# Moving the first dense half's weight conversion from the attention loop to expert slots 1 to 6

## The chip, the cores and the metric

One core of one Trainium2 chip runs the whole program. The metric is the device time in microseconds (us) of one execution; lower is better. Engines are named as the profile names them: PE is TensorE (matmul), PEld its weight load, DVE is VectorE, ACT is ScalarE, POOL is GpSimd, and SP is SyncE, which issues DMAs here. One core shares its DMA engines among all its queues.

## The reference

Three layers follow each other. The inputs of the first two are fp32; the two weight arrays of the last, `w_in` and `w_out`, are fp64.

```python
# attention: 4 batches x 12 heads, 448 tokens, head size 64, causal
scores = mask(scale * (q @ k.T)); attn = softmax(scores); x = attn @ v      # x: [1792, 768]
# mixture of experts: 8 experts, 768 -> 1024 -> 768, one expert for each token
e = argmax(x @ w_gate); gate = softmax(x @ w_gate)[e]
x[t] = gate[t] * (relu(x[t] @ w1[e[t]]) @ w2[e[t]])
# dense layer, 768 -> 2048 -> 768
h = x @ w_in; out = (h - tanh(h)) @ w_out
```

## The kernel before, in words

Every matmul that matters runs on pairs of fp32 tiles: `split` (L152 on ACT for the high part, L154 on DVE for the low part) makes `hi` and `lo`, and three products are summed.

**Attention** goes over 24 pairs of heads. One pass of `for p in range(1, NPAIR + 1)` works on several pairs at once: scores of pair `p` (`attend`), row maxima of pair `p+2` (`rowmax`, a DVE reduction at L489 for each block), turned q and k of pair `p+3` (`turn`, `turn_lo`), and the output of pair `p-1` (`divisor`, `values`, `output`). `divisor` makes `rs`, one over the row sums, on DVE (L568, L570). `output` multiplies the values into PSUM (`po`, L588), evicts them with eight ACT instructions of 112x64 that scale by `rs` (`x_sb`, L595), and evicts the gate logits with two DVE instructions of 112x32 (`tl`, L597). Its PSUM tiles are those that `weigh` and `total` of the next pass need.

**The conversion.** The dense layer's fp64 weights are turned into fp32 by whole-number arithmetic on 32-bit words. The class `Convert` does this in jobs; each has a load (`cv_raw`, SP queue, L96), a `work` step (one ACT square at L108, one POOL compare at L109, three DVE shifts and masks at L110, L112, L114), a `finish` step (one POOL multiply, L126) and a store (SP queue, L135). The first dense half (1024 of the 2048 hidden columns, arrays `win_dr` and `wout_dr[0]` in DRAM) is converted in attention: 42 jobs (18 of 344 or 336 columns, 24 of 256), one in `convert(2p)` and one in `convert(2p+1)` of each pass until they are done. The second half is converted in the dense stage, which the change leaves as it is but for how tiles are got.

**Expert slots.** Tokens are sorted by expert into slots of 128 rows; 18 slots have work here. A slot gathers its rows (POOL, L222), multiplies by `w1` in two halves (`ph0`, `ph1`, L854), applies `relu` (ACT, L859), turns the result (`hturn`, PE L865, then a split), multiplies by `w2` (L874), turns the rows of the next slot (`xturn`), and evicts `ysb` with the gate (ACT, L919), which the next slot stores (POOL, L841). Weights come through four ring buffers `raw0` to `raw3`. `fetch1` loads the next expert's `w1` on the SP queue (L143) where the next change of expert brings one, and then issues, on POOL's queue, four loads of `win_dr` under the condition that the last expert has been reached. `fetch2` does the same for `w2` (L147), with a conditional POOL load of `wout_dr[0]` for the first group. A load whose condition is false moves no bytes, but its engine still waits until the ring buffer is free and the earlier load has landed. `resplit` splits newly loaded weights under a condition read from registers. Expert 0 covers slots 0 to 4; the expert changes at slots 5 and 7 in the stretch that the change touches. After slot 2, `order1` computes tables for the dense layer, most of it on POOL (L998, L1000).

**What sets the order.** The program order of this code is the order on each engine: every engine runs its own list in order, an instruction that waits holds all behind it, and that holds for the queues of SP and POOL too.

**The dense layer** reads the expert output by token, turns it into two tiles `yt` (pool `ytp`, two buffers), and runs both halves. The two `yt` tiles are first written in slot 12.

Of the kernel before, what the change touches and what calls it, by code (L numbers as in the profile page):

```python
# [8 lines left out]
F32 = mybir.dt.float32  # L9
# [18 lines left out]
def fused_kernel(ctx, tc, q, k, v, wg, w1, w2, win, wout, out):  # L28
# [56 lines left out]
    class Convert:  # L85
        def __init__(self, pool, width, same):
            self.pool, self.width, self.same, self.jobs = pool, width, same, []
            self.loaded, self.worked, self.finished, self.stored = 0, 0, 0, 0
            self.raw, self.half, self.res = {}, {}, {}

        def load(self, eng):
            if self.loaded < len(self.jobs):
                src = self.jobs[self.loaded][0]
                raw = self.pool.tile([128, self.width, 2], I32, tag="cv_raw", name="cv_raw")
                raw = raw[:, 0:src.shape[1], :]
                eng.dma_start(out=raw, in_=src)  # L96
                self.raw[self.loaded] = raw
                self.loaded += 1

        def work(self):  # L100
            if self.worked < self.loaded:
# [3 lines left out]
                hi, lo = raw[:, :, 1], raw[:, :, 0]  # L105
                a = self.pool.tile([128, self.width], I32, tag="cv_a", name="cv_a")[:, 0:n]
                m = self.pool.tile([128, self.width], F32, tag="cv_m" if self.same else "cv_h", name="cv_m")[:, 0:n]
                nc.scalar.activation(out=m, in_=hi.bitcast(F32), func=AF.Square)  # L108
# [10 lines left out]
        def finish(self):  # L119
            if self.finished < self.worked:  # L120
                m, a = self.half.pop(self.finished)
                src, dst, on_chip = self.jobs[self.finished]
                h = m
                if not self.same:
                    m = self.pool.tile([128, self.width], F32, tag="cv_m", name="cv_m")[:, 0:src.shape[1]]
                nc.gpsimd.tensor_tensor(out=dst if on_chip else m, in0=h, in1=a.bitcast(F32), op=ALU.mult)  # L126
                self.res[self.finished] = m
                self.finished += 1
# [240 lines left out]
    with ExitStack() as actx:  # L369
        ap1 = actx.enter_context(tc.tile_pool(name="ap1", bufs=1))  # L370
        ap2 = actx.enter_context(tc.tile_pool(name="ap2", bufs=2))
        cvp = actx.enter_context(tc.tile_pool(name="cvp", bufs=2))
        xsp = actx.enter_context(tc.tile_pool(name="xsp", bufs=2))
# [199 lines left out]
        def output(i):  # L573
# [40 lines left out]

        CW = 344
        cv = Convert(cvp, CW, False)
        for kk in range(KD):
            for c0 in range(0, F, CW):
                c1 = min(c0 + CW, F)
                cv.jobs.append((win[kk * 128:(kk + 1) * 128, c0:c1, :],  # L620
                                win_dr[kk * 128:(kk + 1) * 128, c0:c1], False))
        for kk in range(KF):
            for c0 in range(0, DM, 256):
                cv.jobs.append((wout[kk * 128:(kk + 1) * 128, c0:c0 + 256, :],
                                wout_dr[0, kk * 128:(kk + 1) * 128, c0:c0 + 256], False))
        N0 = (B - 1) * H
        cv_by = [max(0, min(len(cv.jobs), n + 3)) for n in range(-4, NHEAD + 2)]

        def convert(n):
            while cv.finished < cv.worked:  # L630
                cv.finish()
            while cv.stored < cv.finished:
                cv.store(nc.sync)
            while cv.worked < cv_by[n]:
                cv.work()
            while cv.loaded < cv_by[n + 2]:
                cv.load(nc.sync)

        e0_t = {}
# [76 lines left out]
        for p in range(1, NPAIR + 1):  # L716
# [7 lines left out]
            maxrow(p + 1)  # L724
            convert(2 * p)
            turn(p + 3, 1)
# [8 lines left out]
            turn_lo(p + 3, 0)  # L735
            convert(2 * p + 1)
            if p + 5 < NPAIR:
# [4 lines left out]
        for n in range(NHEAD - 3, NHEAD):  # L742
            store(n)
        assert cv.stored == len(cv.jobs)

# [40 lines left out]
    with ExitStack() as mctx:  # L786
# [24 lines left out]

# [25 lines left out]
        def slot(s):  # L837
# [86 lines left out]
        def tables():  # L924
# [43 lines left out]
            nc.vector.tensor_copy(rg["more"], hn)  # L968
            nc.vector.tensor_tensor(out=rg["fin"], in0=chg, in1=hn, op=ALU.subtract)

# [71 lines left out]
    with ExitStack() as dctx:  # L1042
        dp = dctx.enter_context(tc.tile_pool(name="dp", bufs=2))
        dio = dctx.enter_context(tc.tile_pool(name="dio", bufs=2))
        pbs = [dio.tile([128, DM], F32, name=f"pb{i}", bufs=1) for i in range(NTT)]
        cv = Convert(dctx.enter_context(tc.tile_pool(name="cvd", bufs=2)), HALF, True)
        assert NHALF == 2
# [205 lines left out]
```

## Time and profile before

| what | us |
|---|---|
| runs before (3), median | 1143.76 (1140.94 to 1148.23) |
| the profiled execution | 1142.36 |
| its span | 1140.9 |
| PE busy in the span | 1069.3 (94%) |
| DVE busy | 776.0 (68%) |
| ACT busy | 590.7 (52%) |
| POOL busy | 481.3 (42%) |
| mean granted clock of the core | 0.982 |

The profiled execution lasts 1.46 us longer than its span; the span runs from the first to the last recorded instruction. Attention's passes fill the stretch from 36 to 301 us of the span, slot 0 the stretch from 301 to 324, slots 1 to 17 follow with some 18.4 us each up to 646, and the dense layer takes the rest. A matmul's record lasts until its modelled end, so a busy PE is not PE at its peak. The granted clock is a share of full speed: 1.00 is 2.4 GHz, and a row between 0.5 and 1.00 mixes both levels.

### The profile page before, as it was taken

What the parts mean: (1) busy time and instruction counts of PE and PEld (TensorE: products, weight loads), DVE (VectorE), ACT (ScalarE), POOL (GpSimd) and SP (SyncE); (2) the same over time, 40 slices, a digit from 0 to 9 for tenths busy, and PEclk for the clock granted to TensorE, in tenths of its full rate; (3) what the DMA queues carried; (4) which work ended last, traced back from release to release, by engine and by line L of the source; (5) the groups of instructions that cost most, each with busy time, mean ns of one, the idle gap of its engine ahead of it and who ended that gap; (6) DMA issues with size and microseconds to landing.
All of it is one profiled execution on the core that took longest, in us unless ns stands there. A gap on an engine that the chain in (4) does not pass through costs nothing. (4 is left out here: it accounts for less than half of the span.)

```text
span 1140.9 us, 22881 instructions
## 1 busy us (share of the span) xinstructions
PE 1069.3 (94%) x7395; PEld 959.1 (84%) x7395; DVE 776.0 (68%) x1824; ACT 590.7 (52%) x1321; POOL 481.3 (42%) x698
## 2 busy tenths in 40 slices
PE   5988898888899999999999899999999999999996
PEld 4665666655698989898888899999999999999996
DVE  5899798986541336516656499889999855556553
ACT  2566565655532445626666565555567644434442
POOL 3688786776313210111112156667675322222221
PEclk9999899998899999999999899999999999999999
DMA  7376576666441367637979453444656422322310
GB/s 163 88 186 188 142 207 152 174 160 200 120 140 56 116 218 250 225 97 231 306 233 308 141 186 126 141 160 159 208 171 238 167 82 85 111 101 67 112 53 32
DMA packets 149203, 179.76 MB, mean 158 GB/s; under 512 B 75344, under 2 KB 118096, under 8 KB 147280
## 3 DMA queue, kind: packets, MB, share of 16 engines
q1 hardware_dynamic: 142816, 148.30, 42.0%
q0 software_dynamic: 6256, 29.90, 7.8%
q8 instruction: 59, 0.97, 0.4%
q14 instruction: 72, 0.59, 0.2%
HBM read 263.49 MB, written 46.80 MB: 272 GB/s over the span
## 5 line engine op out<-in xcount | busy, mean ns | idle before, releaser
L1087 PE MATMUL ph<-yt,w1hi 128*128 128x256 f32 x1344 | 260.7, 284 | 3.3 <-ACTq L1028 3.3
L1124 PE MATMUL po<-w2hi,gg 128*128 128x384 f32 x896 | 247.4, 337 | 1.6 <-DVE gg L154 1.6
L1087 PEld LDWEIGHTS ph<-yt,w1hi 128*128 128x128 f32 x1344 | 217.8, 192 | 3.6 <-ACTq L1028 3.6
L1087 PE MATMUL ph<-yt,w1lo 128*128 128x256 f32 x672 | 190.7, 284 | 0.0
L1124 PEld LDWEIGHTS po<-w2hi,gg 128*128 128x128 f32 x896 | 163.7, 188 | 2.0 <-DVE gg L154 2.0
L1124 PE MATMUL po<-w2lo,gg 128*128 128x384 f32 x448 | 150.0, 335 | 0.0
L854 PE MATMUL ph<-w1hi,xt 128*128 128x512 f32 x432 | 144.9, 403 | 2.4 <-ACT xt L152 2.4
L1087 PEld LDWEIGHTS ph<-yt,w1lo 128*128 128x128 f32 x672 | 129.0, 192 | 0.0
L1105 DVE SCALAR_TENSOR_TENSOR g<-sq,g 128x256 f32<-128x256 f32 x224 | 110.2, 492 | 12.3 <-DVE g L1105 0.5
L489 DVE CUSTOM_DVE_ANT_0 junk<-pa,maskf 128x448 bf16<-128x448 f32 (+1 forms) x192 | 80.6, 420 | 30.1 <-PE pa L482 25.6
L874 PE MATMUL py<-w2hi,hhi 128*128 128x384 f32 x288 | 99.7, 346 | 1.1 <-ACT hhi L152 1.1
L854 PEld LDWEIGHTS ph<-w1hi,xt 128*128 128x128 f32 x432 | 82.4, 191 | 20.3 <-ACT xt L152 2.5
L874 PE MATMUL py<-w2hi,hlo 128*128 128x384 f32 x288 | 97.1, 337 | 2.1 <-DVE hlo L154 2.1
L874 PE MATMUL py<-w2lo,hhi 128*128 128x384 f32 x288 | 96.7, 336 | 0.0
L154 DVE TENSOR_TENSOR hlo<-tp,hhi 128x512 fp32r<-128x512 f32 x36 | 24.8, 689 | 101.2 <-ACTq L833 96.5
L109 POOL TENSOR_SCALAR cv_m<-cv_m 128x256 f32<-128x256 f32 (+3 forms) x82 | 85.5, 1042 | 17.1 <-ACT cv_m L108 10.7
L154 DVE TENSOR_TENSOR w1lo<-raw,w1hi 128x1536 fp32r<-128x1536 f32 (+1 forms) x47 | 71.5, 1540 | 28.2 <-ACT w1hi L152 27.4
L154 DVE TENSOR_TENSOR w2lo<-raw,w2hi 128x1536 fp32r<-128x1536 f32 x40 | 69.9, 1766 | 28.8 <-ACT w2hi L152 28.8
L854 PE MATMUL ph<-w1lo,xt 128*128 128x512 f32 x216 | 85.9, 398 | 0.0
L1124 PEld LDWEIGHTS po<-w2lo,gg 128*128 128x128 f32 x448 | 84.5, 189 | 0.0
L143 POOL DMA_DIRECT2D raw<-win_dr x72 | 6.4, 89 | 160.9 <-DMA raw<-win_dr 71.7
L152 ACT CAST w2hi<-raw 128x1536 fp32r<-128x1536 f32 x40 | 58.4, 1481 | 18.0 <-DMA raw<-in_moe_w_dram 5.8
(676 smaller groups left out, 2321.3 us busy)
## 6 DMA issues: line engine op xcount, KB each, us to landing
raw<-in_moe_w_dram SPq DMA_DIRECT2D x148, 768.0 KB
raw<-win_dr POOLq DMA_DIRECT2D x72, 768.0 KB
raw<-wout_dr POOLq DMA_DIRECT2D x17, 768.0 KB
yt_dr<-yt SPq DMA_DIRECT2D x7, 1536.0 KB
yt<-yt_dr SPq DMA_DIRECT2D x7, 1536.0 KB
y_dr<-ysb POOLq DMA_DIRECT2D x18, 384.0 KB
cv_raw<-in_moe_w_out_dram SPq DMA_DIRECT2D x24, 256.0 KB
cv_raw<-in_moe_w_in_dram SPq DMA_DIRECT2D x24, 256.0 KB
```

What stands on the lines that cost most here:

```text
L109: nc.gpsimd.tensor_scalar(out=m, in0=m, scalar1=TINY * TINY, scalar2=None, op0=ALU.is_ge)
L143: eng.dma_start(out=ring[g].rearrange("p (k f) -> p k f", f=G1), in_=src[:, g * G1:(g + 1) * G1].rearrange("(k p) f -> p k f", p=128), **kw)
L152: nc.scalar.copy(out=dhi, in_=src)
L154: eng.tensor_tensor(out=dlo, in0=src, in1=dhi.bitcast(F32), op=ALU.subtract)
L489: nc.vector.tensor_tensor_reduce(out=junk[:nq, :w], in0=pa[:nq, j, at[c]:at[c] + w], in1=maskf[:nq, m0:m0 + w], scale=1.0, scalar=-3.0e38, ...
L854: nc.tensor.matmul(ph, lhsT=a[:, kk, :], rhs=w[:, kk, z * 512:(z + 1) * 512], start=(kk == 0 and n_ == 0), stop=(kk == KD - 1 and n_ == 2))
L874: nc.tensor.matmul(pys[z], lhsT=a[:, kk, :], rhs=w[:, kk, z * HALF:(z + 1) * HALF], start=(kk == 0 and n_ == 0), stop=(kk == KF - 1 and n_ ...
L1087: nc.tensor.matmul(ph, lhsT=w[:, kk, f * 128:(f + 1) * 128], rhs=yt[:, a, kk, :], start=(kk == 0 and n_ == 0), stop=(kk == KD - 1 and n_ = ...
L1105: nc.vector.scalar_tensor_tensor(out=g, in0=sq, scalar=float(c_), in1=g, op0=ALU.add, op1=ALU.mult)
L1124: nc.tensor.matmul(po_t[ub][tt][z], lhsT=gg[:, a, tt * 128:(tt + 1) * 128], rhs=w[:, f, z * HALF:(z + 1) * HALF], start=(f == 0 and n_ == ...
```

## The change

The 42 jobs leave attention, with their tile pool `cvp`. In their place 48 jobs of 256 columns each are done in slots 1 to 6, eight in a slot, in four calls `convert(s, 2)`: after `hturn(0)`, after `hturn(1)`, after `xturn(s + 1)`, and behind the last resplit. Each call does, twice: `finish` of the job before, `store` of the one before that, `work` of the next, and `load` of the one two ahead. The first two loads are issued at the end of slot 0, behind the four `w1` loads of `fetch1(0)`. The buffers are cut from the two `yt` tiles: four sets of raw, `a` and `m`.

In attention, `output` now evicts `x_sb` with two DVE instructions of 112x2x128 instead of eight ACT instructions of 112x64.

`fetch1` issues POOL's four conditional loads of `win_dr` only from slot `FIN` = 5 on; a condition that would be true in an earlier slot is summed into that of slot 5. `tables` gets one small reduction and two casts for it. The dense stage's conversion gets its tiles by a function; its work is the same.

```diff
             for z, po in enumerate(pos):
                 cs = slice(2 * z, 2 * z + 2)
-                for c in range(2 * z, 2 * z + 2):
-                    for j in range(2):
-                        nc.scalar.activation(out=x_sb[:, c, h0 + j * D:h0 + (j + 1) * D],
-                                             in_=po[:, c % 2, j * D:(j + 1) * D], func=AF.Copy, scale=rs[:, c, j:j + 1])
+                nc.vector.tensor_tensor(out=x_sb[:, cs, h0:h0 + 128].rearrange("p c (j d) -> p c j d", j=2),
+                                        in0=po[:, :, 0:128].rearrange("p c (j d) -> p c j d", j=2),
+                                        in1=rs[:, cs, :].unsqueeze(3).to_broadcast([CP, 2, 2, D]), op=ALU.mult)
...
-            convert(2 * p)
...
-            convert(2 * p + 1)
...
+        cbuf = [ytp.tile([128, 2, KD, TB], F32R, tag="yt", name="yt").rearrange("p a k t -> p (a k t)")
+                for i in range(2)]
...
+        def convert(s, k):
+            for _ in range(k if s >= CV0 else 0):
+                cv.finish()
+                if cv.stored + 1 < cv.finished or cv.finished == len(cv.jobs):
+                    cv.store(nc.sync)
+                cv.work()
+                cv.load(nc.sync)
...
-            f = nc.gpsimd.value_load(rg["fin"][0:1, s:s + 1], min_val=0, max_val=1)
...
-            for g in range(NG1):
-                raw1(g, win_dr, eng=nc.gpsimd, cond=f > 0)
+            if s >= FIN:
+                f = nc.gpsimd.value_load(rg["fin"][0:1, s:s + 1], min_val=0, max_val=1)
+                for g in range(NG1):
+                    raw1(g, win_dr, eng=nc.gpsimd, cond=f > 0)
...
             hturn(0)
+            convert(s, 2)
...
             hturn(1)
+            convert(s, 2)
...
                 xturn(s + 1)
+            convert(s, 2)
             if s == 0:
                 tables()
                 fetch1(s)
+                cv.load(nc.sync)
+                cv.load(nc.sync)
             for g in range(2, NG1):
                 resplit(s + 1, 1, range(g, g + 1))
                 fetch2(s + 1, range(g, g + 1))
+            convert(s, 2)
```

On DVE, in one pass of the attention loop before, the three instructions of a job (L110 to L114) stand ahead of `rs`:

```order
L489 ISA mcol_182 128x1
L110 TENSOR_SCALAR cv_a<-cv_raw 128x336
L112 SCALAR_TENSOR_TENSOR cv_a<-cv_raw,cv_a 128x336
L114 SCALAR_TENSOR_TENSOR cv_a<-cv_raw,cv_a 128x336
L568 TENSOR_SCALAR rs<-pst 112x8
L570 RECIPROCAL rs<-rs 112x8
L467 TENSOR_TENSOR klo<-tp,khi 128x448
```

At the same place after the change (L484, L563, L565, L462 are the lines L489, L568, L570, L467 of before), with the end of the pass, where `x_sb` stands now:

```order
L484 ISA mcol_180 128x1
L563 TENSOR_SCALAR rs<-pst 112x8
L565 RECIPROCAL rs<-rs 112x8
L462 TENSOR_TENSOR klo<-tp,khi 128x448
...
L588 TENSOR_TENSOR x_sb<-po,rs 112x2x128
L591 TENSOR_TENSOR tl<-po,rs 112x32
L588 TENSOR_TENSOR x_sb<-po,rs 112x2x128
L591 TENSOR_TENSOR tl<-po,rs 112x32
L462 TENSOR_TENSOR qlo<-tp,qhi 128x448
```

The job between `mcol` and `rs` is gone, and so is the one that followed `qlo`; two evictions of `po` stand between the `tl` instructions.

On ACT in slot 1 before, the second `relu` (the second row of L859) follows directly on the split of the first turned half:

```order
L859 ACTIVATE hs<-ph 128x512
L152 CAST hhi<-tp 128x512
L859 ACTIVATE hs<-ph 128x512
L833 COMPARE_AND_BRANCH
L152 CAST w1hi<-raw_74 128x6x256
L833 UNCONDITIONAL_BRANCH x2
L152 CAST hhi<-tp 128x512
```

On ACT in slot 1 after the change (L860, L148, L834 are L859, L152, L833 of before; `yt` is the name of the conversion's tiles):

```order
L860 ACTIVATE hs<-ph 128x512
L148 CAST hhi<-tp 128x512
L107 ACTIVATE yt<-yt 128x256 x2
L860 ACTIVATE hs<-ph 128x512
L834 COMPARE_AND_BRANCH
L148 CAST w1hi<-raw_74 128x6x256
L834 UNCONDITIONAL_BRANCH x2
L148 CAST hhi<-tp 128x512
L107 ACTIVATE yt<-yt 128x256 x2
```

The squares of the first two jobs now stand ahead of the second `relu` of the slot, and two more behind each later step.

On SP's queue at the end of slot 0 and the start of slot 1 after the change, where the conversion's loads (L95) stand behind the four `w1` loads, and further on between the two groups of a `w2` load:

```order
L139 DMA raw_74<-in_moe_w_dram 128x6x256
...
L139 DMA raw_77<-in_moe_w_dram 128x6x256
L95 DMA yt<-in_moe_w_in_dram 128x512 x4
L803 TENSOR_LOAD nxt_i
...
L143 DMA raw_74<-in_moe_w_dram 128x2x768
L131 DMA win_dr<-yt 128x256
L95 DMA yt<-in_moe_w_in_dram 128x512
L131 DMA win_dr<-yt 128x256
L95 DMA yt<-in_moe_w_in_dram 128x512
L143 ISA
L143 DMA raw_75<-in_moe_w_dram 128x2x768
```

Two of the four loads in the L95 row are slot 0's, two are slot 1's first call. The store of each job (L131) stands on the same queue, between weight loads.

On POOL in slot 1 after the change, where the conditional load of `wout_dr` (L143 there, L147 before) stands between the compares (L108) and the multiplies (L122):

```order
L842 DMA y_dr<-ysb 128x768
L108 TENSOR_SCALAR yt<-yt 128x256
L122 TENSOR_TENSOR yt<-yt 128x256
L108 TENSOR_SCALAR yt<-yt 128x256
...
L143 DMA raw_74<-wout_dr 128x2x768
L122 TENSOR_TENSOR yt<-yt 128x256
L108 TENSOR_SCALAR yt<-yt 128x256
```

The multiply of the second job stands behind a DMA issue that waits for the ring buffer.

## Rows read from the trace of the kernel before

**Rows 1.** Stages: length, busy (count) of PE, PEld, DVE, ACT, POOL; clock, DMA, GB/s

```profile
36.00:262.00 226.00, 198.27 (x1779) 139.34 (x1777) 200.26 (x621) 140.19 (x363) 176.26 (x253) 0.97 0.63 168
301.00:324.00 23.00, 22.40 (x125) 19.09 (x126) 17.65 (x49) 9.62 (x13) 5.71 (x6) 0.86 0.36 114
646.00:1140.90 494.90, 483.96 (x3432) 483.29 (x3432) 368.28 (x856) 249.70 (x665) 216.30 (x232) 0.99 0.38 132
```

**Rows 2.** Waits of PE in attention's passes: us in total, times, longest us

```profile
PE po L588 <- DVE rs L568: 10.6, 18, 0.9
PE pa L482 <- DVE mcol L489: 8.4, 11, 2.0
PE pa L482 <- DVE tl L597: 5.5, 16, 0.7
```

**Rows 3.** Windows of single attention passes, with the columns of rows 1

```profile
113.62:129.29 15.67, 13.66 (x90) 10.44 (x92) 11.01 (x40) 7.34 (x19) 10.00 (x15) 0.67 0.55 152
161.39:171.90 10.51, 9.59 (x90) 6.68 (x92) 9.48 (x31) 6.95 (x18) 8.00 (x12) 1.00 0.83 222
171.90:185.32 13.42, 11.62 (x95) 7.75 (x97) 11.82 (x43) 6.86 (x20) 8.57 (x13) 0.87 0.52 124
262.15:274.98 12.83, 11.29 (x80) 7.71 (x82) 9.59 (x35) 6.20 (x16) 8.45 (x14) 0.73 0.83 274
```

**Rows 4.** Lines by shape, 36 to 262 us: busy us, mean ns, idle before

```profile
L595 ACT ACTIVATE x_sb<-po,rs 112x64 f32<-112x64 f32 x160 | 35.2, 331 | 13.2 <-DVE rs L570 12.1 <-issue 0.6 <-PE po L588 0.4
L112 DVE SCALAR_TENSOR_TENSOR cv_a<-cv_raw,cv_a 128x256 int32<-128x256 int32 x22 | 21.2, 965 | 0.8
L110 DVE TENSOR_SCALAR cv_a<-cv_raw 128x256 int32<-128x256 int32 x22 | 15.5, 704 | 0.5 <-DMA cv_raw<-in_moe_w_out_dram 0.5
L114 DVE SCALAR_TENSOR_TENSOR cv_a<-cv_raw,cv_a 128x256 int32<-128x256 int32 x22 | 12.2, 554 | 0.8
L597 DVE TENSOR_TENSOR tl<-po,rs 112x32 f32<-112x32 f32 x40 | 7.1, 183 | 5.0 <-ACT x_sb L595 4.0
```

**Rows 5.** Lines by shape in the dense layer, 650 to 880 us, columns as in rows 4

```profile
L109 POOL TENSOR_SCALAR cv_m<-cv_m 128x256 f32<-128x256 f32 x24 | 22.4, 934 | 5.6 <-ACT cv_m L108 3.6
L1101 DVE TENSOR_TENSOR th<-ph,th 128x256 f32<-128x256 f32 x53 | 21.9, 414 | 0.0
L126 POOL TENSOR_TENSOR raw<-cv_m,cv_a 128x256 f32<-128x256 f32 x24 | 18.5, 770 | 3.9 <-DVE cv_a L114 3.9
L112 DVE SCALAR_TENSOR_TENSOR cv_a<-cv_raw,cv_a 128x256 int32<-128x256 int32 x24 | 10.2, 425 | 0.8
```

**Rows 6.** Timeline of slot 1, by engine: start us, us, instruction, [idle before]

```profile
328.07 3.14 SPq L143 DMA_DIRECT2D raw<-in_moe_w_dram  x4
...
332.93 0.06 POOL L143 DMA_DIRECT2D raw<-win_dr  x1 [14.87 <-DMA raw<-in_moe_w_dram]
...
340.17 0.04 POOL L143 DMA_DIRECT2D raw<-win_dr  x1 [2.08 <-DMA raw<-in_moe_w_dram]
...
332.89 0.60 ACT L859 ACTIVATE hs<-ph 128x512 f32<-128x512 f32 x1 [2.22 <-PE ph L854]
...
334.73 0.60 PE L865 MATMUL tp<-ident,hs 128*128 128x128 f32 x4
```

**Rows 7.** Windows of slots 1, 2, 4 and 6, with the columns of rows 1

```profile
341.00:361.10 20.10, 19.09 (x104) 17.05 (x103) 4.21 (x13) 4.29 (x9) 3.45 (x14) 1.00 0.27 80
361.10:379.50 18.40, 18.40 (x102) 16.81 (x101) 2.80 (x5) 4.72 (x9) 12.61 (x26) 1.00 0.14 43
398.00:416.40 18.40, 17.43 (x95) 15.63 (x94) 10.30 (x9) 9.11 (x11) 1.89 (x5) 1.00 0.94 311
435.00:453.00 18.00, 18.00 (x100) 16.40 (x99) 11.12 (x10) 9.76 (x12) 1.74 (x6) 1.00 1.00 338
```

**Rows 8.** Timeline of POOL between the expert changes, columns as in rows 6

```profile
396.96 0.04 POOL L147 DMA_DIRECT2D raw<-wout_dr  x1 [8.85 <-DMA raw<-wout_dr]
...
410.17 0.04 POOL L143 DMA_DIRECT2D raw<-win_dr  x1 [9.77 <-DMA raw<-in_moe_w_dram]
```

More of the change, by code (lines that the diff above doesn't have):

```diff
@@ L85, in fused_kernel, with __init__ @@
     class Convert:
-        def __init__(self, pool, width, same):
-            self.pool, self.width, self.same, self.jobs = pool, width, same, []
+        def __init__(self, tiles):
+            self.tiles, self.jobs = tiles, []
             self.loaded, self.worked, self.finished, self.stored = 0, 0, 0, 0
@@ L93, in load @@
                 src = self.jobs[self.loaded][0]
-                raw = self.pool.tile([128, self.width, 2], I32, tag="cv_raw", name="cv_raw")
-                raw = raw[:, 0:src.shape[1], :]
+                raw = self.tiles(self.loaded, "cv_raw", src.shape[1])
                 eng.dma_start(out=raw, in_=src)
@@ L105, in work @@
                 hi, lo = raw[:, :, 1], raw[:, :, 0]
-                a = self.pool.tile([128, self.width], I32, tag="cv_a", name="cv_a")[:, 0:n]
-                m = self.pool.tile([128, self.width], F32, tag="cv_m" if self.same else "cv_h", name="cv_m")[:, 0:n]
+                a = self.tiles(self.worked, "cv_a", n)
+                m = self.tiles(self.worked, "cv_m", n)
                 nc.scalar.activation(out=m, in_=hi.bitcast(F32), func=AF.Square)
@@ L122, in finish @@
                 src, dst, on_chip = self.jobs[self.finished]
[L123 to L126, printed above, removed]
+                nc.gpsimd.tensor_tensor(out=dst if on_chip else m, in0=m, in1=a.bitcast(F32), op=ALU.mult)
                 self.res[self.finished] = m
@@ L613, in store @@
                 in_=xs.pop(n // XH))
[L615 to L625, printed above, removed]
-        N0 = (B - 1) * H
[L627 to L637, printed above, removed]
+        N0 = (B - 1) * H
         e0_t = {}
@@ L743, in fused_kernel @@
             store(n)
-        assert cv.stored == len(cv.jobs)
     SOON, LATE = 1, 3
@@ L796, in fused_kernel, with cve_tile @@
         xts.append([mp.tile([128, KD, 128], F32R, name=f"xt1{z}", bufs=1) for z in range(2)])
+        CW = 256
+        CV0, CVN = 1, 8
+        cbuf = [ytp.tile([128, 2, KD, TB], F32R, tag="yt", name="yt").rearrange("p a k t -> p (a k t)")
+                for i in range(2)]
+        def cve_tile(j, nm, n):
+            o = (j // 2 % 2) * 4 * CW
+            t = cbuf[j % 2]
+            if nm == "cv_raw":
+                return t[:, o:o + 2 * n].bitcast(I32).rearrange("p (f t) -> p f t", t=2)
+            o += 2 * CW if nm == "cv_a" else 3 * CW
+            return t[:, o:o + n].bitcast(I32 if nm == "cv_a" else F32)
+        cv = Convert(cve_tile)
+        for kk in range(KD):
+            for c0 in range(0, F, CW):
+                cv.jobs.append((win[kk * 128:(kk + 1) * 128, c0:c0 + CW, :],
+                                win_dr[kk * 128:(kk + 1) * 128, c0:c0 + CW], False))
+        CVW = len(cv.jobs)
+        for kk in range(KF):
+            for c0 in range(0, DM, CW):
+                cv.jobs.append((wout[kk * 128:(kk + 1) * 128, c0:c0 + CW, :],
+                                wout_dr[0, kk * 128:(kk + 1) * 128, c0:c0 + CW], False))
+        FIN = CV0 + -(-(CVW + 2) // CVN)
+        assert FIN < SMIN and CV0 + -(-(len(cv.jobs) + 2) // CVN) < SMIN - 3
+        def convert(s, k):
[5 more added lines that the diff above has]
+                cv.load(nc.sync)
         def regs(s):
@@ L968, in tables @@
             nc.vector.tensor_copy(rg["more"], hn)
-            nc.vector.tensor_tensor(out=rg["fin"], in0=chg, in1=hn, op=ALU.subtract)
+            fi = row("fi")
+            nc.vector.tensor_tensor(out=fi, in0=chg, in1=hn, op=ALU.subtract)
+            fs = be[:, 0:1]
+            nc.vector.tensor_reduce(out=fs, in_=fi[:, 0:FIN + 1], axis=AX.X, op=ALU.add)
+            nc.vector.tensor_copy(rg["fin"], fi)
+            nc.vector.tensor_copy(rg["fin"][:, FIN:FIN + 1], fs)
         vals = mp.tile([CP, NC, 3, NCT], F16, name="vals", bufs=1)
@@ L1015, in fused_kernel @@
             slot(s)
+            if s == SMIN - 3:
+                assert cv.stored == len(cv.jobs)
             if s == 2:
@@ L1045, in fused_kernel, with cvd_tile @@
         pbs = [dio.tile([128, DM], F32, name=f"pb{i}", bufs=1) for i in range(NTT)]
-        cv = Convert(dctx.enter_context(tc.tile_pool(name="cvd", bufs=2)), HALF, True)
+        cvd = dctx.enter_context(tc.tile_pool(name="cvd", bufs=2))
+        def cvd_tile(j, nm, n):
+            shape = [128, HALF, 2] if nm == "cv_raw" else [128, HALF]
+            return cvd.tile(shape, F32 if nm == "cv_m" else I32, tag=nm, name=nm)[:, 0:n]
+        cv = Convert(cvd_tile)
         assert NHALF == 2
```

3 lines of the change are left out of this document (removed).

## The prediction

> **What bounds the kernel now.** I read the windows by stage first. In the attention passes PE is busy 198.27 of 226.00 us and DVE 200.26; neither fills the stretch, and DVE has more work than PE [rows 1]. In slot 0 PE is busy 22.40 of 23.00 us [rows 1], and in the later slots it has next to no gaps: 18.40 of 18.40 us in slot 2, 18.00 of 18.00 in slot 6 [rows 7]. So a microsecond freed in attention can be won, and a microsecond in which a slot makes PE wait is lost in full. The table of PE's waits says what the gaps in attention are: 10.6 us for `rs`, 8.4 us for the row maxima, 5.5 us for `tl`, all DVE instructions [rows 2]: 24.5 us, in waits of under 2 us each. Third, single passes: an even one lasts 10.51 us with PE busy 9.59, at clock 1.00; three others lasted 15.67, 13.42 and 12.83 us at a mean clock of 0.67, 0.87 and 0.73 [rows 3]. Their PE busy time grew too, so part of them ran at the lower level, 1.2 GHz.
>
> **What attention gains.** A job of 256 columns costs DVE 0.704 + 0.965 + 0.554 = 2.22 us [rows 4], so two jobs a pass take 4.4 us of DVE's 9.5 to 11 us [rows 3]. They leave. Two evictions of `x_sb` come. The trace of before has no DVE instruction of that shape; the nearest rows are `tl` at 0.183 us for 32 elements [rows 4] and an eviction of 128x256 at 0.414 us [rows 5]. The new one has 256 elements, so I take 0.41, 0.8 us a pass; the ends are 0.4 and, if the broadcast factor doubles it, 1.7. DVE is left with some 6 to 7 us in a pass of 10. A job stands directly ahead of `rs` in the order, and one behind `qlo` ahead of the next row maxima, so the waits in rows 2 lose what stands before their releaser. I take nine tenths of 24.5 us: 22. The rest stays, since DVE still has to turn `pst` into `rs` after PE has written it. ACT loses 8 x 0.331 = 2.6 us a pass and with it the 12.1 us in which it waited for `rs` [rows 4]; that ACT is off PE's path in this stage, so I add 2 us for waits of PE that rows 2 do not name. The low-clock passes cost 13.66 - 9.59 = 4.1, 11.62 - 9.59 = 2.0 and, for 80 matmuls of a usual 90, 11.29 - 8.5 = 2.8 us of PE time [rows 3], together 8.9. Each followed gaps of PE; with fewer gaps I let 6 go. Sum: -30 us, bounds -18 (half of the waits are taken over by POOL or PE's own chain, no clock won) and -42 (all 24.5, all 8.9, and a pass that also gets shorter behind them).
>
> **What the slots lose.** 48 jobs come. A job costs ACT a square, POOL 0.934 + 0.770 = 1.70 us [rows 5], and DVE between 2.22 us [rows 4] and about 1.0, if all three instructions shrink as L112 does from 0.965 to 0.425 away from attention [rows 4, 5]. I take 1.3, nearer to the quiet row, since the slots are quiet. Eight jobs add 10 us of DVE to slots with 2.8 to 11.1 us of DVE and 14 us of POOL to slots with 1.7 to 12.6 us of POOL [rows 7]. By busy time each slot of 18.4 us could hold that but for one: slot 2, with `order1` in it, hands its POOL work on, and 12.6 + 13.6 = 26 us do not go into 18.4. What matters is the order.
>
> Slot 1. The first two loads stand on SP's queue behind four `w1` loads issued from 328.07 on. Those landed in order at 332.93 and later, the last at 340.17, as POOL's released waits show [rows 6]. The conversion's first load lands behind them, at 340.5 to 341. On ACT its square stands ahead of the second `relu`, which ran at 332.89, and PE's second turn, at 334.73 before [rows 6], needs that `relu`. Square, square and `relu` end near 342.5, so PE turns at some 343: 8 us late. In a gap of that size I expect a stretch at 1.2 GHz, as slot 0 has at 0.86 after attention's last gaps (0.14 of 23 us, 3.2 us) [rows 1]; 3 us. In return POOL no longer waits for those landings in slots 1 to 4, and the 1.0 us in which PE was idle in slot 1 (19.09 of 20.10, [rows 7]) goes. Slot 1: +10. Below, 0, if the load is served beside the weights; above, 13.
>
> The row is that of loads that land one after the other, some 2.2 us apart (332.93 to 340.17 for four). The Trainium skill says in "DMA: Bandwidth & Descriptors", section "Queues, rings and completion order", that descriptors of a ring are taken in order, yet that a later transfer may finish its writes before an earlier one. The in-order landings agree with the first half; nothing here shows the second. By the second half slot 1 would cost nothing and the sum would be 10 lower.
>
> Boundaries of slots 3 to 6. Three chains cross here. POOL's `finish` stands behind `order1` (slots 2 to 3) and behind conditional loads that wait for weights to land: 8.85 us in one case and 9.77 us in another [rows 8]. SP's store waits for that `finish`, and the next conversion load and the next weight group stand behind the store on SP's queue. ACT's squares for the late job stand ahead of the next slot's split, of `ysb` and of the next `relu`, which PE needs. Before, POOL's waits there cost nothing, as only a gather stood behind them. Now, from slot 3 into 4, 4 into 5, 5 into 6 and 6 into 7, a wait of 8.85 or 9.77 us can reach PE; of it, what the four jobs in flight and the slack of a slot's eighth of its work cover is left out. I take 5 us each, near the middle between 0 (all is covered) and 10 (the whole wait reaches PE): +20. The added transfers, 48 of 256 KB in and 128 KB out, are 18.9 MB over 110 us, 172 GB/s, beside 43 to 338 GB/s [rows 7]; two of the slots already have a DMA share of 0.94 and 1.00 [rows 7], so late landings there are more likely than early ones. The casts in `tables` are 4 small DVE instructions beside PE's work in slot 0: nothing, and 1 us if they are not covered.
>
> **The sum.** The profiled execution, 1142.36 us, is 1.4 us below the median shown; -30 + 10 + 20 gives 1142.4, and on the median's level some 1143. The tail of attention and the dense layer are unchanged.
>
> **Rivals.** A: the slots hide all but slot 1's wait. For it: PE needs nothing from a job; slots have 7 to 15 us of free DVE [rows 7]; SP and POOL work ahead by four sets. Against: the shares of 0.94 and 1.00 and the 9.77 us [rows 7, 8]. Time: 1142.4 - 30 + 10 = 1122. B, on the slower side: SP's queue becomes the bound in slots 3 to 6. A store waits for a POOL multiply that waits behind a conditional load for weights that a transfer on SP's own queue brings, so the weights of the next expert come late and PE waits for their split; from the point at which a boundary costs over 8 us it is this, and four boundaries of 10 us give 1142.4 - 30 + 10 + 40 = 1162. For it: the landings of rows 8 and the full DMA share. Against: `fetch2` of most slots moves no bytes. C: attention gains more. If a pass is not bound by PE's 9.59 us but follows DVE and ACT down, as PEld's 6.68 us would allow [rows 3], a pass of 9.2 us gives another 24 x 0.35 = 8 us: 1134 with the slots as forecast. The Trainium skill, "Perfetto Trace Analysis", section "Identifying the Most-Contended Engine", says that matmul busy time is a poor measure of the headroom and that the share of weight loads is a better one; by it PE has more room here than 9.59 of 10.51 shows. The rows bear that out only in that PEld is lower; they do not show a pass at 9.2. D: attention gains only 15, because a POOL or ACT wait takes each DVE wait's place: 1142.4 - 15 + 30 = 1157. Against it: POOL and ACT lose work too in that stage.
>
> **Chances.** Forecast 0.40, with a range of its own from 1131 to 1154; A 0.25, C 0.08, B 0.20, D 0.07. A measurement of this kernel tells a change from none at about 1%, 11.4 us. Faster by over 1% (under 1132.3): A and C, 0.33. Slower by over 1% (over 1155.2): B and D, 0.27. Within: 0.40. The range reaches from A's 1122, less 4 for a slot 1 that is shorter than I think, to B's 1162 and 2 more: 1118 to 1164.
>
> **What would show it.** In attention: waits of PE for DVE, 24.5 us before, fall under 5, an even pass falls to about 9.6 us, and fewer passes lie at a clock below 1.00. If passes stay at 10.5, D is right; at 9.2, C. In slot 1: ACT's first square in slot 1 waits some 7 us for a DMA and the second turn on PE starts 8 us late; a square that starts on time there refutes that term. In slots 3 to 6: PE waits for ACT's `xt`, `w1` splits or `ysb`, and ahead of that waits for a store or `finish` on SP and POOL; slots of 18.4 us there mean A, slots of 28 us B. The forecast as a whole is wrong if the attention stage ends less than 18 us earlier than at 301, or if slots 1 to 7 together are less than 15 us longer.

## The result and the profile after

The changed kernel took 1160.43 us (median of 4, 1159.07 to 1162.22) against 1143.59 us before: 1.0144 times as long, 95% interval 1.0107 to 1.018. It is slower by 17 us where no change was forecast; the time itself lies in the range given. Its profiled execution has a span of 1157.5 us and a mean clock of 0.957 (1140.9 us and 0.982 before).

The 17 us are the difference of two amounts that are both about twice what was forecast. The first is in attention. One window spans the 24 passes in each trace, from one start of the copy of values to another. In the kernel before (columns as in rows 1):

```profile
38.70:296.30 257.60, 223.11 (x1971) 155.85 (x1967) 217.75 (x668) 157.59 (x411) 197.41 (x284) 0.95 0.62 168
```

In the changed kernel, the same window, and one pass of it:

```profile
37.10:242.30 205.20, 198.97 (x1975) 148.31 (x1975) 143.08 (x589) 103.10 (x185) 115.79 (x200) 1.00 0.47 118
...
99.64:108.46 8.82, 8.82 (x92) 6.61 (x92) 6.39 (x27) 4.55 (x9) 5.03 (x10) 1.00 0.75 176
```

The stage is 52.4 us shorter. PE's idle time in it fell from 34.5 to 6.2 us, and its busy time from 223.1 to 199.0. A pass lasts 8.82 us (10.51 in [rows 3]) and PE has no gap left in it. PE's waits in 36 to 301 us, in the columns of [rows 2]; the first row is no longer attention but slot 1, which starts 55 us earlier now:

```profile
PE tp L866 <- ACTq L834: 9.6, 1, 9.6
PE pv L532 <- DVE tl L591: 2.3, 2, 1.9
...
PE pa L477 <- DVE mcol L484: 0.3, 1, 0.3
```

The 24.5 us of [rows 2] are down to 2.6. DVE's two evictions cost what was taken for them (columns as in rows 4):

```profile
L588 DVE TENSOR_TENSOR x_sb<-po,rs 112x256 f32<-112x256 f32 x48 | 19.6, 408 | 0.0
```

The second amount is in slots 1 to 7. A slot is cut here where PE starts the first `w1` product of it (L854 before, L855 now), so that each holds the same work of PE, some 100 matmuls. Slots 1 to 7 took 129.4 us before, one by one 18.0, 19.4, 18.0, 18.1, 19.7, 18.2 and 18.0:

```profile
324.00:453.40 129.40, 127.42 (x703) 115.07 (x702) 49.45 (x73) 52.17 (x73) 23.49 (x70) 1.00 0.51 166
```

In the changed kernel slots 1 to 7, each by itself, answer to [rows 7] (whose windows are nearly those of slots 2, 3, 5 and 7; the title of that group and the prediction count them one too low):

```profile
268.50:297.90 29.40, 19.79 (x101) 17.92 (x100) 14.14 (x45) 6.33 (x14) 9.53 (x13) 0.83 0.65 210
297.90:316.00 18.10, 18.10 (x99) 16.35 (x98) 12.85 (x25) 6.76 (x15) 12.71 (x17) 1.00 0.62 193
316.00:345.20 29.20, 18.96 (x101) 16.19 (x99) 14.72 (x36) 6.97 (x16) 22.82 (x33) 0.91 0.35 112
345.20:373.20 28.00, 24.03 (x98) 20.03 (x99) 18.07 (x33) 10.30 (x19) 15.08 (x21) 0.79 0.57 169
373.20:404.40 31.20, 23.44 (x116) 19.43 (x115) 24.90 (x35) 15.59 (x22) 16.68 (x21) 0.78 0.94 304
404.40:432.20 27.80, 22.47 (x104) 18.77 (x101) 16.98 (x32) 10.06 (x18) 15.02 (x24) 0.82 0.60 181
432.20:462.70 30.50, 22.41 (x99) 18.77 (x98) 20.13 (x24) 14.39 (x19) 14.73 (x18) 0.78 0.84 265
```

They sum to 194.2 us, 64.8 more. Only slot 2 has PE without a gap; in all PE is idle for 45.0 us where it was idle for 2.0, and the clock column falls to between 0.78 and 0.91 in six of seven. PE's busy time for the same work is 149.2 us against 127.4. So of the 64.8 us, 43.0 are new gaps and 21.8 a longer busy time. The clock column is below 1.00 in the six slots where PE's busy time grew, and 1.00 in slot 2, where it did not; so most of the 21.8 are matmuls at the lower level of the clock. A part can be records that overlap less beside gaps, as in attention, and no row splits the two. The balance: the 24 passes -52.4 us; the start before them and slot 0 -3.1 (slot 1 starts at 268.5, before at 324.0: -55.5 in all); slots 1 to 7 +64.8; later slots +6.0; the dense layer +1.3: +16.6, as between the spans.

Where the gaps come from is told by ACT's waits from 262 to 470 us:

```profile
ACT yt L107 <- DMA yt<-in_moe_w_in_dram: 46.8, 17, 13.1
ACT yt L107 <- DMA yt<-in_moe_w_out_dram: 20.5, 10, 6.0
...
ACT yt L107 <- POOL yt L108: 7.9, 2, 6.4
ACT yt L107 <- POOL yt L122: 6.4, 4, 3.6
```

81.6 us in which ACT stood before 33 of the 48 squares (L107), 67.3 of them for loads, with PE's next `relu` or split queued behind. Part of that is covered: in slot 2 ACT stood 7.6 us before squares and PE lost nothing. Of PE's own 45.0 us these are the waits for a `relu` (`hs`) and for the split of newly landed weights:

```profile
PE tp L866 <- ACT hs L860: 10.3, 5, 3.1
...
PE ph L855 <- ACT w1hi L148: 7.3, 2, 4.0
```

The other two large ones, 9.6 and 8.4 us, are followed here. Slot 1 is the place of [rows 6]; SP's queue, ACT and PE in the changed kernel:

```profile
274.15 3.36 SPq L139 DMA_DIRECT2D raw<-in_moe_w_dram  x4
277.56 4.49 SPq L95 DMA_DIRECT2D yt<-in_moe_w_in_dram  x4
...
287.50 0.44 ACT L107 ACTIVATE yt<-yt 128x256 f32<-128x256 f32 x1 [12.27 <-DMA yt<-in_moe_w_in_dram]
288.09 0.43 ACT L107 ACTIVATE yt<-yt 128x256 f32<-128x256 f32 x1 [0.16 <-DMA yt<-in_moe_w_in_dram]
288.43 0.58 ACT L860 ACTIVATE hs<-ph 128x512 f32<-128x512 f32 x1
...
289.06 1.12 PE L866 MATMUL tp<-ident,hs 128*128 128x128 f32 x4 [9.61 <-ACTq L834]
```

The reader sees the four `w1` loads, the conversion's loads behind them, ACT waiting 12.27 us, and PE's second turn after 9.61 us of nothing. Its matmuls there last 1.12 us for four, 0.60 in [rows 6]. Slot 3 shows the other chain, POOL, SP and ACT:

```profile
327.38 9.82 POOL L1012 TENSOR_SCALAR sel<-ioth,o_cpp 112x128 f16<-112x128 f16 x16
...
339.05 0.76 POOL L122 TENSOR_TENSOR yt<-yt 128x256 f32<-128x256 f32 x1
...
339.84 0.34 SPq L131 DMA_DIRECT2D win_dr<-yt  x1
340.29 0.43 SPq L95 DMA_DIRECT2D yt<-in_moe_w_in_dram  x1
...
344.04 0.43 ACT L107 ACTIVATE yt<-yt 128x256 f32<-128x256 f32 x1 [13.13 <-DMA yt<-in_moe_w_in_dram]
344.65 0.86 ACT L148 CAST xt<-tp 128x384 fp32r<-128x384 f32 x2 [0.17 <-ACTq L834]
```

`order1` on POOL, then the multiply, then the store, then the load that needs the stored buffer, then the square, and behind it the split that PE waits for (the waits of PE, 300 to 360 us):

```profile
PE ph L855 <- ACT xt L148: 8.4, 1, 8.4
```

In slot 4 a conditional load that moves no bytes does what `order1` does here (POOL, answering to [rows 8]); the `w2` load ahead of it in the same ring buffer is issued on SP's queue 4.65 us before it is released:

```profile
368.01 0.39 SPq L143 DMA_DIRECT2D raw<-in_moe_w_dram  x1
...
372.66 0.05 POOL L143 DMA_DIRECT2D raw<-wout_dr  x1 [8.77 <-DMA raw<-wout_dr]
```

### The profile page after: what moved, and what is told of

The parts are those of the page before. It is cut to its first block, busy times and chain, and to the rows that moved or that the text cites. A ratio compares the mean times of both kernels' runs of the same rounds, so it can differ in the third digit from the quotient of the medians.

```text
span 1157.5 us, 22709 instructions
## 1 busy us (share of the span) xinstructions
PE 1068.6 (92%) x7395; PEld 965.8 (83%) x7395; DVE 773.1 (67%) x1893; ACT 552.7 (48%) x1135; POOL 481.6 (42%) x690
## 5 line engine op out<-in xcount | busy, mean ns | idle before, releaser
L855 PE MATMUL ph<-w1hi,xt 128*128 128x512 f32 x432 | 156.0, 429 | 22.5 <-ACT xt L148 9.2
L855 PEld LDWEIGHTS ph<-w1hi,xt 128*128 128x128 f32 x432 | 88.6, 206 | 44.1 <-ACT xt L148 9.6
L484 DVE CUSTOM_DVE_ANT_0 junk<-pa,maskf 128x448 bf16<-128x448 f32 (+1 forms) x192 | 80.8, 421 | 58.5 <-PE pa L477 53.5
L855 PE MATMUL ph<-w1lo,xt 128*128 128x512 f32 x216 | 91.6, 424 | 4.8 <-DVE w1lo L150 3.5
L515 POOL TENSOR_SCALAR_AFFINE_SELECT pT<-pT 128x256 f32<-128x256 f32 x96 | 37.2, 388 | 103.7 <-ACT pT L511 96.0
L511 ACT ACTIVATE pT<-ps 128x896 f32<-128x896 f32 (+2 forms) x72 | 53.2, 739 | 51.0 <-PE ps L509 49.8
L148 ACT CAST w2hi<-raw 128x1536 fp32r<-128x1536 f32 x40 | 58.1, 1479 | 17.4 <-DMA raw<-in_moe_w_dram 6.0
```

The costliest lines, as they stand in the source:

```text
L148: nc.scalar.copy(out=dhi, in_=src)
L484: nc.vector.tensor_tensor_reduce(out=junk[:nq, :w], in0=pa[:nq, j, at[c]:at[c] + w], in1=maskf[:nq, m0:m0 + w], scale=1.0, scalar=-3.0e38, ...
L511: nc.scalar.activation(out=pT[:, :, o0:o1], in_=ps[:, :, 0:o1 - o0], func=AF.Exp, scale=0.125)
L515: nc.gpsimd.affine_select(out=pT[p0:, :, o:o + nk], in_=pT[p0:, :, o:o + nk], pattern=[[0, 2], [1, nk]], compare_op=ALU.is_ge, fill=0.0, b ...
L855: nc.tensor.matmul(ph, lhsT=a[:, kk, :], rhs=w[:, kk, z * 512:(z + 1) * 512], start=(kk == 0 and n_ == 0), stop=(kk == KD - 1 and n_ == 2))
```

## The experiments

The theory: attention is held by the order on DVE, and the conversion is what stands in it; the slots are held by chains of instructions in order (POOL multiply, SP store, SP load, ACT square, then what PE needs). Its rivals: the eviction of `x_sb`, or POOL, held attention; the bytes themselves, or the sum of engine work, hold the slots. Each run was timed beside the kernel before on its own chip (medians 1143.8 to 1146.4 us), and a ratio is to that. Two runs are best compared by their ratios, whose intervals reach some 0.2 to 0.6% (2 to 7 us) to either side; a difference of 3 to 5 us between two runs is not clear of noise.

**Eviction alone (e1).** The kernel before, with only the DVE eviction of the diff.

> The kernel before with one part of the change alone: x_sb evicted by two DVE instructions instead of eight of ACT; the conversion stays in attention. Theory (attention's gain comes from the conversion that leaves DVE and POOL): DVE gets 0.8 us more a pass, passes stay at 10.3 to 11 us, 1136 to 1150. Rival (the eviction by ACT, 2.6 us a pass, was what held PE's PSUM tiles): passes fall towards 9.5 us, 20 us or more are gained, under 1124.

1147.1 us, ratio 1.0011 (0.9985 to 1.0036): the theory. The 24 passes take 257.3 us, as before. PE's waits there, against [rows 2]:

```profile
PE pa L482 <- DVE mcol L489: 23.9, 37, 2.1
PE po L588 <- DVE rs L568: 3.0, 11, 0.4
```

The wait for `rs` fell from 10.6 to 3.0 us and that for the row maxima rose from 8.4 to 23.9: the releaser's name changed, the sum hardly did (26.9 us, 24.5 in [rows 2]). Both are the same queue of DVE work.

**Eviction undone (e2).** The changed kernel with the eviction of before (the first block of the diff reversed).

> The changed kernel with x_sb evicted by ACT as before; the conversion stays in the slots. Theory: passes stay near 8.8 us, at most 0.5 us longer since ACT's eviction takes 2.6 us where DVE's takes 0.8: 1158 to 1172. Rival (the eviction is half of the gain): passes of 9.8 us or more, 24 us lost, over 1180.

1157.3 us (1.0112 times before, 1.0075 to 1.0149), and the 24 passes take 206.6 us, 1.4 more than in the changed kernel. One pass:

```profile
127.52:136.35 8.83, 8.83 (x92) 6.61 (x92) 5.13 (x23) 6.16 (x18) 4.98 (x10) 1.00 0.39 91
```

So the eviction has next to no part in the gain.

**DVE's part of the conversion left out (e9)** of the kernel before:

```diff
                 nc.gpsimd.tensor_scalar(out=m, in0=m, scalar1=TINY * TINY, scalar2=None, op0=ALU.is_ge)
-                nc.vector.tensor_scalar(out=a, in0=hi, scalar1=3, scalar2=0x3FFFFFFF,
+                if self.same:
+                    nc.vector.tensor_scalar(out=a, in0=hi, scalar1=3, scalar2=0x3FFFFFFF,
...
```

> The kernel before with the conversion left in attention but without its three DVE instructions a job (the stored weights of the first half are then the square's mask alone, so the output is not the reference's); loads, ACT's square, POOL's two instructions and the stores stay. Theory (DVE's order is what held attention: a job ahead of rs and of the row maxima): passes of 8.8 to 9.2 us instead of 10.5 and more, the stage 40 to 52 us shorter, 1093 to 1106. Rival (POOL, ACT or the transfers of the conversion hold PE): less than 15 us gained, over 1130.

1105.94 us, ratio 0.9641 (0.9584 to 0.9698): 40 us less, at the edge of what the theory gave. The 24 passes take 218.7 us, 38.9 less than before (40 to 52 expected), with DVE's busy time down from 217.75 to 134.90.

**POOL's and ACT's part left out (e11)**, the same edit on the square, the compare and the multiply.

> The kernel before with the conversion left in attention but without ACT's square and POOL's two instructions a job (the masking of tiny weights in the first half is left out); loads, DVE's three instructions and the stores stay. Theory (DVE holds attention): passes stay at 10.2 us or more, at most 10 us gained, 1135 to 1147. Rival (POOL's 3.4 us and ACT's 0.9 us a pass hold it): over 20 us gained, under 1125.

1130.48 us, ratio 0.9854 (0.9795 to 0.9914): between the two. The 24 passes take 244.4 us, 13.2 less. PE still waits for DVE as in [rows 2], 7.6, 6.9 and 6.7 us, and DVE's own instructions got shorter: the row of [rows 4] with 704 ns reads

```profile
L111 DVE TENSOR_SCALAR cv_a<-cv_raw 128x256 int32<-128x256 int32 x24 | 9.8, 410 | 8.3 <-DMA wout_dr<-cv_a 6.0 <-DMA win_dr<-cv_a 2.2
```

38.9 and 13.2 add up to 52.1, the whole gain of the stage (52.4; 51.0 in e2, where the conversion alone has left). So some three quarters are DVE's part and a quarter that of POOL and ACT, some of it through DVE. No run leaves out both parts and keeps the transfers, so that they add is inferred.

**No conversion (e7).** The changed kernel with the calls of `convert` empty and two plain copies early in attention.

> The changed kernel without the conversion of the first half anywhere; in its place win_dr and wout_dr[0] are filled early in attention by two plain copies of w1 and w2 of expert 0, so the output is not the reference's. It prices the whole conversion in the slots. Theory: slots 1 to 7 take 129 us as before instead of 194, the attention gain stays, 1160 - 65 = 1095 or, if the later slots lose their 6 us too, 1089. Rival (slots are slow for another reason, such as attention's earlier end or the clock): over 1110.

1107.8 us, ratio 0.9664 (0.9608 to 0.972). The copies held attention's first loads: the first copy of values starts at 49.45 us instead of 37.1, so some 12 of the 13 to 19 us over the expectation are the experiment's own. What it was made for is clear: slots 1 to 7 take what they took before,

```profile
283.30:412.50 129.20, 127.74 (x705) 115.44 (x704) 50.28 (x78) 52.40 (x73) 23.09 (x50) 1.00 0.52 166
```

and the conversion in the slots costs 65 us, low clock included. The later slots stay 6 us longer than in the one trace of before: 194.9 us against 189.2. In the trace of e1, whose slots are those of before, they took 191.9, so part of that lies between executions.

**Two loads first (e3).**

```diff
             if s == 0:
+                cv.load(nc.sync)
+                cv.load(nc.sync)
                 tables()
                 fetch1(s)
-                cv.load(nc.sync)
-                cv.load(nc.sync)
```

> The changed kernel with the conversion's first two loads issued in slot 0 ahead of the four w1 loads instead of behind them. Theory (each loss is an in-order chain): ACT's first square in slot 1 no longer waits 12.27 us for its load, PE's 9.61 us wait ahead of the second turn goes and with it the low clock behind it, so 10 to 13 us less than the changed kernel's 1160: 1147 to 1150, and slots 3 to 6 stay as they are. Rival (the added transfers themselves make the slots slow, whatever their order): the w1 weights land later in exchange, under 5 us of gain, over 1155.

1157.48 us, ratio 1.0105 (1.007 to 1.014), 3 us less than the changed kernel: the rival's number, but not by its mechanism. The square that waited 12.27 us did not wait, and the wait for the next two jobs took its place: their loads are issued in slot 1 and so stand behind the same `w1` loads.

```profile
289.87 0.43 ACT L107 ACTIVATE yt<-yt 128x256 f32<-128x256 f32 x1 [6.92 <-DMA yt<-in_moe_w_in_dram]
```

Slot 1 went from 29.4 to 20.6 us and slot 2 from 18.1 to 23.2: most of the loss moved on by a slot.

**`order1` later (e4).**

```diff
-            if s == 2:
+            if s == 7:
                 order1()
-            if s == 5:
+            if s == 9:
                 order2()
```

> The changed kernel with order1 after slot 7 instead of slot 2 (and order2 after slot 9). Theory: POOL's 11.5 us of tables no longer stand ahead of a finish, ACT's 13.13 us wait in slot 3 and PE's 8.4 us wait at the start of the next slot go, with the low clock behind them: 12 to 17 us less, 1143 to 1148. Rival (transfers or the sum of added engine work): slot 3 stays at about 35 us, within 4 us of 1160.

1155.12 us, ratio 1.0083 (1.005 to 1.0115), 5 us less, between theory and rival. Slots 3 and 4 are what the theory said:

```profile
318.40:337.70 19.30, 18.21 (x99) 16.30 (x98) 13.91 (x27) 7.06 (x15) 13.45 (x18) 1.00 0.61 182
337.70:361.00 23.30, 20.32 (x100) 17.39 (x99) 16.58 (x29) 10.11 (x18) 12.75 (x16) 0.93 0.64 190
```

57.2 us became 42.6. But `order1` in slot 8 holds the store of `ysb` on POOL, and slots 8 and 9 took 44.3 us against 38.1. ACT's row there:

```profile
ACT ysb L926 <- DMA y_dr<-ysb: 6.6, 1, 6.6
```

**POOL's empty loads out (e5).**

```diff
+        FIN = 8
...
-                f = nc.gpsimd.value_load(rg["fst"][0:1, s:s + 1], min_val=0, max_val=1)
+                f = None
+                if s >= SMIN:
+                    f = nc.gpsimd.value_load(rg["fst"][0:1, s:s + 1], min_val=0, max_val=1)
...
-                if g < SOON:
+                if g < SOON and s >= SMIN:
```

> The changed kernel without POOL's conditional loads of wout_dr ahead of slot 14 (they never bring bytes there, since at least 14 slots are used) and with win_dr's from slot 8 on instead of 5. Theory: in slots 4 to 6 a finish waits on POOL behind such an issue for 8.8 us; without it the slots of 28, 31 and 28 us lose 5 to 9 us each: 15 to 27 us less, 1133 to 1145. Rival (DMA share of 0.65 to 0.9 in these slots is the limit): under 6 us of gain, over 1154.

1145.73 us, 15 less than the changed kernel, at the lower end of the theory and level with the kernel before (0.9999, 0.9977 to 1.002). Slots 4 to 6:

```profile
346.90:373.60 26.70, 23.44 (x98) 18.99 (x99) 17.70 (x32) 10.31 (x19) 16.78 (x20) 0.84 0.62 183
373.60:402.30 28.70, 22.28 (x115) 17.75 (x114) 26.83 (x37) 15.61 (x22) 20.93 (x19) 0.88 0.98 323
402.30:426.20 23.90, 19.75 (x107) 16.38 (x102) 16.86 (x31) 10.20 (x18) 15.56 (x18) 1.00 0.68 208
```

79.3 us instead of 87.0, and slot 7 took 28.0 instead of 30.5; slots 4 to 6 still take 23 more than the 56.0 before. The waits for the loads themselves remain.

**All three (e6).**

> The three edits of the runs before it together. Theory: the gains add, 40 to 55 us less than 1160, 1105 to 1120, and the attention gain of about 52 us stays whole, so that it is 2 to 3.5% faster than the kernel before. Rival (transfers or added engine work limit the slots): the gains don't add, over 1140.

1130.69 us, ratio 0.9872 (0.9838 to 0.9905): 30 us less, short of the forecast 40 to 55. The gains of the three do add: by the ratios 0.39, 0.61 and 1.45% alone, 2.45 in all, and 2.72% together, which is within the intervals. What was too large in the forecast were the gains themselves, two of them above all: 3 and 5 us where 10 to 13 and 12 to 17 were expected. It is faster than both kernels. Slots 1 to 7 take 166.5 us, and ACT still waits for loads in every one of them.

**More sets (e8).** Six sets of buffers in the same two tiles, whose last third lay unused, and loads four jobs ahead.

```diff
-            o = (j // 2 % 2) * 4 * CW
+            o = (j // 2 % 3) * 4 * CW
...
-                cv.load(nc.sync)
+                if cv.loaded < cv.worked + 4:
+                    cv.load(nc.sync)
```

> The three edits together (1130.7) with six sets of buffers instead of four in the same two tiles, loads four jobs ahead instead of two, and four loads in slot 0 ahead of the w1 loads. Theory: what is left of the slots' loss is ACT waiting in order for a load issued only one call before; with it gone slots 2 and 3 fall from 20 to 21 us to about 18.5 and slots 4 to 6 from 25 to 26 us to about 20: 1100 to 1112. Rival (the DMA share of 0.73 to 0.95 in slots 4 to 6 is the limit): less than 8 us, over 1122.

1119.55 us, ratio 0.977 (0.9719 to 0.9821): 11 us less, between theory and rival. Slots 1 to 7 take 155.3 us; slots 4 and 6 fell from 20.9 and 23.6 us to 19.7 each, and the expert change in slot 5 did not fall, with the DMA engines and DVE both nearly full:

```profile
349.30:378.80 29.50, 23.69 (x99) 19.84 (x98) 28.08 (x42) 12.88 (x21) 23.61 (x21) 0.83 0.98 329
```

**Six jobs a slot (e10)**, in slots 1 to 8, `order1` and `order2` after slots 9 and 10.

> The kernel with six sets and all edits (1119.6) with six jobs a slot in slots 1 to 8 instead of eight in slots 1 to 6 (one job after each hturn's first call and in the last call, two in the others), order1 after slot 9 and order2 after slot 10. Theory (what is left is ACT's square waiting for a load that arrives behind weights): fewer jobs a slot hide it better, slots 1 to 8 lose 12 us less together: 1104 to 1112. Rival (the bytes of the expert changes and the conversion together are what slots 1, 5 and 7 wait for): within 5 us of 1119.6.

1116.52 us, ratio 0.9732 (0.9673 to 0.979). 3 us: the rival's number. Slots 5 and 7 take 24.2 us each, and what PE waits for longest there (3.1 us) is DVE's low part of newly landed weights, not a transfer:

```profile
348.90:373.10 24.20, 20.34 (x100) 17.34 (x99) 22.94 (x31) 12.00 (x19) 19.74 (x16) 0.93 0.97 319
...
PE ph L859 <- DVE w1lo L150: 3.1, 1, 3.1
```

DVE is busy for 22.94 of the 24.20 us, so its work fills these slots, beside a DMA share of 0.97; no run takes away one of the two and keeps the other. The 24.4 us that the next expectation gives for slot 1 count up to the late `ysb`: slot 1 takes 18.1 us here, and slot 2, behind it, 22.2.

**From slot 2 on (e12).**

```diff
-        CV0, CVN = 1, 6
+        CV0, CVN = 2, 7
...
-            convert(s, 1)
+            convert(s, 2)
```

> The kernel with six jobs a slot (1116.5), with the conversion in slots 2 to 8, seven jobs a slot, instead of 1 to 8; the first four loads stay at the end of slot 0, the next come only after the w1 loads of slot 0 have landed. Theory (slot 1's loss is the conversion's loads standing behind those w1 loads): slot 1 falls from 24.4 to about 18.5 us, and the whole to 1108 to 1113. Rival (the wait moves to slots 2 and 3, as it moved within slot 1 when two loads were put first): within 3 us of 1116.5.

1112.64 us, ratio 0.9726 (0.9696 to 0.9757): the theory's range, but the ratio is that of e10 (0.9732), so no gain over e10 is shown. Slots 1 and 2 are free of loss, 36.3 us against 40.3 in e10 (slot 2 of e10 and of this run):

```profile
290.40:312.60 22.20, 19.80 (x99) 17.51 (x98) 9.84 (x23) 7.36 (x17) 11.62 (x14) 0.92 0.61 183
...
289.40:307.60 18.20, 18.20 (x101) 16.46 (x100) 7.44 (x17) 6.88 (x16) 7.46 (x9) 1.00 0.34 108
```

But slots 5 and 7, with seven jobs, take 25.6 us each instead of 24.2, and slots 1 to 9 together 187.1 against 187.4: what slot 2 gained the later slots lost, as the rival has it, only further on. It has the lowest median here, 2.7% faster than the kernel before.

## Why the prediction was wrong

**Attention, forecast -30, measured -52.4, and -55.5 with slot 0.** The mechanism was right: e9 and e11 show that DVE's part of the conversion carries 38.9 of 52.4 us, and the eviction's 0.41 us an instruction measured 0.408. What failed is the size of the gain, in PE's busy time. The forecast took nine tenths of 24.5 us of named waits and 2 us of others, 24 in all, and PE's idle time fell by 28.3. It let 6 us of busy time go, all for the low clock, and PE's busy time fell by 24.1. A busy PE of 9.59 us was not its need: without gaps the same pass needs 8.82. 24 passes at 9.59 - 8.82 = 0.77 us are 18.5, and with the 8.9 us of low clock 27.4, a little more than the 24.1 measured; not every pass was that of [rows 3]. Rival C had this direction, at 9.2 us a pass and 8 us, and had both its chance and its size too low. The rule of the Trainium skill in "Perfetto Trace Analysis", section "Identifying the Most-Contended Engine", that matmul busy time misleads, is borne out: PEld's 6.61 us hardly differs from the 6.68 in [rows 3], while PE's busy time fell by 0.77.

**Slot 1, forecast +10.** This term was right in mechanism and size: slot 1 took 29.4 us against 18.0, +11.4, and slots 1 and 2 together 47.5 against 37.4, +10.1. The chain was right to the instruction: a square that waits for a load behind the `w1` loads, and a turn on PE 9.61 us late (8 in the forecast), then matmuls at the lower clock. The 1.0 us of idle PE that the forecast booked as won in slot 1 was slot 2's, by the count of slots above, and was won there. e3 shows why the order of two loads is no cure, and e12 that slots 1 and 2 are free of loss once the conversion starts in slot 2. By the rule of the Trainium skill in "DMA: Bandwidth & Descriptors", section "Queues, rings and completion order", that a later transfer may finish first, the term could have been 0; here ACT waited 12.27 us for the load behind the weights, and no row shown has one that overtakes.

**Boundaries of slots 3 to 6, forecast +20.** This is the step that failed and turned the sign. Slots 3 to 7 took 146.7 us against 92.0, +54.7: 11.2, 9.9, 11.5, 9.6 and 12.5, five slots and not four boundaries. The three chains named are there (`order1`, POOL's empty loads, SP's store ahead of the load), but 5 us each was chosen as the middle between 0 and the wait, and 9.6 to 12.5 us reached PE. Three things were left out of it or wrong. The slack assumed to cover part of a wait is small: with buffers for four jobs and loads one call ahead ACT waits for the load before 27 of 48 squares; the 7.6 us of such waits in slot 2 cost PE nothing, those behind `order1` and empty loads did. The gaps cost twice: PE's busy time grew by 21.8 of the 64.8 us in slots 1 to 7, mostly at the lower clock, which the forecast counted for slot 1 alone, at 3. And the sum of busy time was wrong: the forecast says that each slot but one could hold its jobs, but eight jobs at its 1.3 us are 10.4 us, and beside 10.30 and 11.12 us of DVE [rows 7] that is 20.7 and 21.5 in slots of 18.4. Of these two windows one, slot 5, has jobs; there DVE was busy for 24.90 us. Of the parts, e4 prices `order1` at 14.6 us in slots 3 and 4, e5 POOL's empty loads at 7.7 us in slots 4 to 6 and 2.5 in slot 7 (15 in the whole). e6 leaves 37.1 of the 64.8 us, and e8's buffers and distance take 11.2 of these. What is left from there on lies mostly in the slots of the expert changes, 5 and 7, where DVE and the DMA engines are both nearly full; which of them sets the length stays open, though PE's waits name DVE.

**The sum.** -30 + 30 became -55.5 + 64.8, with 6.0 in later slots and 1.3 in the dense layer. The two errors hid each other in the total; that the time lies in the range is luck. Rival B, on the slower side at +20, was the nearest: its store behind a POOL wait is real, its price of 10 us a boundary was right, and its chance of 0.20 too low. Its late weights are a part only: PE's waits for the split of new `w1` weights on ACT are 7.3 of 45.0 us. What argued against it, that most of `fetch2` moves no bytes, was no argument: it is the waiting of an empty load that costs.

Open: the 6 us in the later slots, which e7 has as well; which part of POOL's and ACT's 13.2 us in attention acts through DVE's shorter instructions and which through POOL's own order; and whether DVE or the bytes hold slots 5 and 7 in the last versions. No run splits these.

## What to carry to other kernels

Where an in-order engine serves the bounding engine, a helper's instruction there costs what it may wait for, not what it lasts: look for the longest chain of waits that ends in it (here multiply, store, load, square), and put buffers and distance into that chain before moving work to it. Don't take a stage's PE busy time as its floor while it has gaps, and price every new gap twice, once as idle time and once as matmuls at the lower clock behind it. Add up every engine's busy time slot by slot, old work and new: here DVE was over the slot's length where the experts change. A stretch in which the table of engines shows free time is free only for work whose data are already there.

## What the runs showed of the hardware

- PE's busy time for the same work grows with gaps: a pass of 90 to 92 matmuls at clock 1.00 shows 9.59 us of busy PE with gaps [rows 3] and 8.82 without. It counts overlapping records once. The `pv` matmuls of 128x448 last 564 ns in both passes, while of those that PE had to wait for the mean is longer (before, then after):

```profile
L482 PE MATMUL pa<-khi,qhi 64*128 64x448 f32 x2 | 0.5, 454 | 0.3 <-DVE tl L597 0.3
...
L477 PE MATMUL pa<-khi,qhi 64*128 64x448 f32 x2 | 0.4, 356 | 0.0
```

- Gaps and the lower clock together, in these slots: the same 703 matmuls take 127.4 us of busy time at a mean clock of 1.00, and 149.2 us beside 45.0 us of gaps, at 0.78 to 1.00 by slot.
- DVE's instructions on 32-bit words got shorter when POOL's compare and multiply and ACT's square of the conversion left attention (e11): from 704 [rows 4] to 410 ns, from 554 to 461, but from 965 only to 868. Which of the two engines does it no run shows.
- A conditional DMA that moves nothing held POOL for 8.77 us, until 372.66, with the load ahead of it in the same ring buffer issued at 368.01.
